# k'v with its operands swapped and two head pairs side by side in TensorE's columns, with other due times for the stages

## The chip, the cores and the metric

The kernel runs on one core of a Trainium2 chip. The metric is the device time of one execution in microseconds (us), here the median of several runs on the chip. The working views are those of one profiled execution: its page, its groups of instructions, its timeline, its windows of busy time and the chain of work that ended last.

## The reference, cut to what matters

Inputs are q, k and v of shape (4, 4, 1088, 32) (batch, heads, sequence, head dimension), two sketches S1 and S2 of shape (8, 32), and four weight matrices. The attention is linear, with 64 features for each head:

```python
def phi(x):                                   # r = 8, so 64 features
    a = einsum('rd,bhsd->bhsr', S1, x)
    b = einsum('rd,bhsd->bhsr', S2, x)
    return einsum('bhsi,bhsj->bhsij', a, b).reshape(..., 64)
q_p, k_p = phi(q), phi(k)
kv = einsum('bhsf,bhsd->bhfd', k_p, v)        # "k'v": 64 x 32 for each head
z = sum(k_p, axis=2)
x = (einsum('bhsf,bhfd->bhsd', q_p, kv) / (einsum('bhsf,bhf->bhs', q_p, z)[..., None] + 1e-06))
# then, with x as (batch, 1088, 128):
theta = x @ w_theta
y = einsum('ts,bsd->btd', w_tok_r, x * cos(theta)) + einsum('ts,bsd->btd', w_tok_i, x * sin(theta))
u = x + y
out = u + maximum(u @ w_ch, 0)
```

## The kernel before

The sequence is padded to nine chunks of 128 positions, in three groups of three chunks (`NG` = 3, `GC` = 3). Four batches go through the same stages, and each operation carries the name of its stage: `keysB` (loads, the k slices, sums for the denominators), `valuesB` (k features and k'v), `queriesB` (q slices, features, denominators), `mixedB` (numerators, the division, theta, cosine and sine) and `mixingB` (the token mixing with the two 1088 x 1088 matrices, the channel product and the output). The token matrices arrive as 64-bit words in 34 pieces of 544 columns (`w_tok` into `st`), and each piece is turned into float32 (`wT`) by three ScalarE activations (`step`, `step`, `wT`) and two VectorE operations (stage `weights`). These `wT` rows are the moving operands of every batch's mixing: 17 rows in three column groups of 384, 384 and 320, float32.

Nothing is issued in the order in which it is written. `Order.note` records every operation with an estimated duration, and `Order.lay_out` writes the orders of PE, DVE, ACT and SP out in advance: it walks a clock for each engine, takes among the operations that could start within `WAIT` of each other the one with the earliest due time, and allots the buffers. Due times run backwards from the ends; `SOONER` shifts them by stage (a negative number lets a stage come later), and the rows of the mixing get theirs from `START`, `PACE` and 0.65 a row. For PE the planner also follows a guess of the clock gate (an exponential average of PE's use, with two thresholds). Since all operations are issued from one helper, every instruction of the profile carries the same line (L319 before, L320 after), and they are told apart by the tiles they write and read. The engines themselves work through their written order and wait where an operand is late.

The step that is changed is `keys_values(b)`, stage `valuesB`. For each chunk and each pair of heads n it multiplies the k features of two heads (`kp` in the buffer `feat`, 128 positions x 128 features, the stationary operand) with the v of two heads (`vn` in a buffer `big`, 128 positions x 64, moving) and sums over the nine chunks in one PSUM bank, `kv[:, n]`, 128 features x 64. Two ScalarE copies then put the two diagonal blocks into `kvbd[b % 2]`, the block-diagonal operand of `numerator(b, g)`. In the profile each float32 product is two matmul instructions with two weight loads; k'v is the group `w<-big,feat`, 72 products and 144 instructions in all. The other names that matter: `fT` and `ks` (k or q features on their way), `ksl` and `qsl` (16-bit slices), `lv` (features for the denominators), `kvbd`, `xT`, `tn` and `tt` (mixed), `uT` and `ot` (output), `hmTq` (a small constant operand, used once early).

Of the kernel before, what the change touches and what calls it, by code (L numbers as in the profile page):

```python
# [32 lines left out]
P = 128  # L33
# [3 lines left out]
ROUND = 1.5 * 2.0**23  # L37
TWO_PI = 6.2831850
TINY = 2.0**-60
START = 90, 130, 170, 215  # L40
BIG = 5

SOONER = {"keys1": 20, "keys3": 15, "mixed0": 10, "mixed1": 20, "mixed3": 15, "mixing0": -20,
          "mixing1": -30, "mixing2": -25, "queries0": -5, "queries1": -5, "queries2": -10,
          "queries3": 5, "values1": 20, "values2": 25, "values3": 35}
ST = 6
PACE = 2.5
PIECE = 544
# [64 lines left out]
class Order:  # L113
# [3 lines left out]

    WAIT = 0.05  # L120

    def __init__(self, nc):
        self.nc, self.ops, self.due, self.tags, self.stage = nc, [], math.inf, {}, None
# [25 lines left out]
    def duration(self, engine, call, out, ins):  # L149

        n = math.prod(out.shape[1:])
        psum = any(isinstance(x, View) and x.buf.tag == "w" for x in ins)
        if engine == "DVE":
            if call == "tensor_reduce":
                n = math.prod(ins[0].shape[1:])
            if call == "reciprocal":
                return 0.29, 0.1
            own = any(isinstance(x, View) and x.shape[1:] == (1,) for x in ins[1:])
            fast = call in ("tensor_scalar", "tensor_copy", "memset") and not psum
            return 0.09 + n / (1920 if fast and not own else 1400 if fast else 970), 0.1  # L160
        if engine == "ACT":
            wide = any(isinstance(x, View) and x.buf.tag == "st" for x in ins)
            own = any(isinstance(x, View) and x.shape[1:] == (1,) for x in ins[1:])
            return 0.05 + 0.07 * own + n / (900 if out.dtype != F32 and wide else 1020 if wide else 1130), 0.15
        if engine == "SP":
            return 0.36, 0.0
        if call == "transpose":
            return 0.11, 0.3
        if ins[0].dtype == F32:
            return max(0.22, n / 600), 0.3  # L170
        return max(0.06, n / 2400), 0.3

    def note(self, engine, fn, call, a, kw):
# [38 lines left out]
    def lay_out(self):  # L212
        ops = self.ops
        self.dues()
        left, after = [len(op.behind) for op in ops], [[] for _ in ops]
        for op in ops:
            for n in op.behind:
                after[n].append(op.n)
        bufs = []
        for op in ops:  # L220
            for b in op.bufs:
                if b.uses[0] == op.n:
                    bufs.append(b)
        by_tag = {}
        for b in bufs:
            b.left = len(b.uses)
            by_tag.setdefault(b.tag, []).append(b)
        free = {tag: [0.0] * len(x[0].slots) for tag, x in by_tag.items()}
        waiting = {tag: list(x) for tag, x in by_tag.items()}
        live = {tag: [] for tag in by_tag}  # L230
        done = [False] * len(ops)

        def safe(b):

            if waiting[b.tag][0] is b:
                held = live[b.tag]
                if len(held) == 0:
                    return True
            events = []
            for x in live[b.tag] + [b]:  # L240
                events.append((max(n for n in x.uses if not done[n]), 1, -1))
            for x in waiting[b.tag]:
                if x is not b:
                    events += [(x.uses[0], 0, 1), (x.uses[-1], 1, -1)]
            count = len(live[b.tag]) + 1
            if count > len(b.slots):
                return False
            for _, _, d in sorted(events):
                count += d
                if count > len(b.slots):  # L250
                    return False
            return True

        clock = dict(PE=0.0, DVE=0.0, ACT=0.0, SP=0.0)
        ready = {e: [] for e in clock}
        at = [0.0] * len(ops)
        for op in ops:
            if not left[op.n]:
                ready[op.engine].append(op)
        link, use, used, slow = 0.0, 0.0, 0.0, True  # L260
        out, self.log = [], []
        while len(out) < len(ops):
            best = None
            for e, rs in ready.items():
                starts = []
                for op in rs:
                    t = max(clock[e], at[op.n])
                    for b in op.bufs:
                        if b.slot is None:
                            since = [x for x in free[b.tag] if x is not None]  # L270
                            t = max(t, min(since)) if since else math.inf
                    starts.append((t, op))
                while True:
                    first = min((t for t, _ in starts), default=math.inf)
                    if first == math.inf:
                        break
                    t, op = min(((t, o) for t, o in starts if t <= first + self.WAIT),
                                key=lambda x: (x[1].due, x[1].n))
                    if all(b.slot is not None or safe(b) for b in op.bufs):
                        if best is None or t < best[0]:  # L280
                            best = t, op
                        break
                    starts.remove((t, op))
            t, op = best
            e = op.engine
            for b in op.bufs:
                if b.slot is None:
                    b.slot = min((x, i) for i, x in enumerate(free[b.tag]) if x is not None)[1]
                    free[b.tag][b.slot] = None
                    waiting[b.tag].remove(b)  # L290
                    live[b.tag].append(b)
            cost = op.cost
            if e == "PE":
                use = use * math.exp(-(t - used) / 4.0)
                slow = use < (0.6 if slow else 0.3)
                cost *= 2.0 if slow else 1.0
                use, used = 1 - (1 - use) * math.exp(-cost / 4.0), t + cost
            end = clock[e] = t + cost
            if e == "SP":
                link = end = max(end + 1.6, link) + op.bytes / 290e3  # L300
            self.log.append((e, t, end, op))
            ready[e].remove(op)
            out.append(op)
            done[op.n] = True
            for b in op.bufs:
                b.left -= 1
                b.end = max(getattr(b, "end", 0.0), end + op.late)
                if not b.left:
                    free[b.tag][b.slot] = b.end
                    live[b.tag].remove(b)  # L310
            for n in after[op.n]:
                o = ops[n]
                at[n] = max(at[n], end if o.engine == e == "PE" else end + op.late)
                left[n] -= 1
                if not left[n]:
                    ready[o.engine].append(o)
        for op in out:
            r = [x.real() if isinstance(x, View) else x for x in op.args]
            op.call(*r, **{k: x.real() if isinstance(x, View) else x for k, x in op.kw.items()})  # L319
# [3 lines left out]
def kernel(  # L323
# [12 lines left out]
    B, _, NC, H, D = q.shape  # L336
# [113 lines left out]
    t_ = psum()  # L450
    T.transpose(t_[:2 * H, :P], View(hm.buf, hm.buf.slots[0]), ident)
    A.activation(hmT, t_[:2 * H, :P], AF.Copy, scale=512.0)
    hmTq = buf("hmTq", [P, P])[:H]
    t_ = psum()
    T.transpose(t_[:H, :P], hm, ident)
    A.activation(hmTq, t_[:H, :P], AF.Copy, scale=512.0)
# [81 lines left out]
    kvbd = []  # L538
# [139 lines left out]
    def keys_values(b):  # L678

        vn = tiles["v", b]  # L680
        kv = psum()[:, :4 * D].rearrange("p (n d) -> p n d", n=2)
        for g in range(NG):
            ks = tiles["kf", b, g]
            kp = buf("feat", [P, CH, R, R], F32, 2)
            tt(V, kp, ks[:, :, 0:R].unsqueeze(3).to_broadcast([P, CH, R, R]),
               ks[:, :, R:2 * R].unsqueeze(2).to_broadcast([P, CH, R, R]), ALU.mult)
            for i in range(GC):
                for n in range(2):
                    c = g * GC + i
                    T.matmul(  # L690
                        kv[:, n], kp[:, i * H + 2 * n:i * H + 2 * n + 2].rearrange("p h i j -> p (h i j)"),
                        vn[:, c, 2 * n:2 * n + 2].rearrange("p h d -> p (h d)"),
                        start=(c == 0 and n == 0), stop=(c == NC - 1), skip_group_check=True)
        for j in range(2):
            pj = slice(j * R * R, (j + 1) * R * R)
            A.copy(kvbd[b % 2][pj, :, j * D:(j + 1) * D], kv[pj, :, j * D:(j + 1) * D])


    NT = NC * HR
# [316 lines left out]
```

## Time and profile before

| | |
|---|---|
| median of 11 runs | 305.98 us (304.55 to 307.21) |
| the profiled execution | 305.75 us, its span 303.6 us |
| PE busy | 261.8 us (86%), 1347 matmuls |
| DVE busy | 227.1 us (75%) |
| ACT busy | 167.2 us (55%) |
| granted TensorE clock, mean | 0.906 |
| k'v, `w<-big,feat` | 144 matmuls, 20.7 us busy |

The page gives shares over the whole span, but the kernel has two parts: up to about 143 us the engines prepare batches and convert the token matrices, and afterwards PE works through the mixing. A share of the whole span therefore tells little; the windows and the chain do. Starts in the timeline matter more than the lengths of matmuls, since matmuls overlap: one float32 matmul of 64 columns is listed with 275 ns, while the next starts 112 ns after it.

### The profile page before, as it was taken

How to read it: one execution, taken by the hardware profiler on the slowest of the kernel's cores; microseconds unless marked ns; L12 is line 12 of the kernel's file. 1: busy time of each engine (PE TensorE's matmuls, PEld its weight loads, DVE VectorE, ACT ScalarE, POOL GpSimd, SP SyncE). 2: the span in 40 equal slices, each digit the busy share in tenths (PEclk: the TensorE clock that was granted, in tenths of full speed). 3: DMA queues.
4: the chain of work that ended last, by engine and by line, in shares of the span. 5: the costliest groups of instructions: out<-in, count | busy, mean ns of one | idle time of the engine just before them, and what ended most of it. 6: DMA issues, size and time to landing. Idle time of an engine off the chain costs nothing.

```text
span 303.6 us, 4008 instructions
## 1 busy us (share of the span) xinstructions
PE 261.8 (86%) x1347; PEld 188.3 (62%) x1347; DVE 227.1 (75%) x646; ACT 167.2 (55%) x334; POOL 0.7 (0%) x6
## 2 busy tenths in 40 slices
PE   4739688743987999488999999999999999999993
PEld 3528576533874656256966676687668766666661
DVE  5999897989699898999999894999789752000121
ACT  4696647598479999999864315325934162000000
POOL 0000000000000000000000000000000000000000
PEclk9958758785597999869999999999999999999998
DMA  7980456658001476752200001000100000000011
GB/s 271 408 339 2 166 189 188 212 154 287 0 2 54 125 266 189 276 201 73 80 1 0 2 26 28 1 1 22 28 26 2 22 0 26 2 0 26 2 46 48
DMA packets 11603, 28.77 MB, mean 95 GB/s; under 512 B 1216, under 2 KB 5568, under 8 KB 11584
## 3 DMA queue, kind: packets, MB, share of 16 engines
q1 hardware_dynamic: 11584, 28.53, 27.6%
q8 instruction: 10, 0.16, 0.2%
q14 instruction: 9, 0.07, 0.1%
HBM read 26.30 MB, written 2.23 MB: 94 GB/s over the span
## 4 chain that ended last, share of the span: by engine, by line
PE 68%; ACT 16%; DVE 10%; DMA 3%; issue 1%; ACTq 0%; DVEq 0%
PE w L319 68%; ACT step L319 7%; ACT wT L319 3%; ACT big L319 2%; ACT lv L319 2%; DMA st<-w_tok 2%; DVE big L319 1%; DMA big<-k_l 1%; DVE wT L319 1%; ACT fT L319 1%; DVE feat L319 1%; DVE m L319 1%; DVE cut_r L319 1%; DVE cut_z L319 1%; DVE ksl L319 0%
## 5 line engine op out<-in xcount | busy, mean ns | idle before, releaser
L319 PE MATMUL w<-wT,st 128*128 128x384 f32 (+1 forms) x384 | 134.2, 482 | 5.0 <-DVE st L319 2.5
L319 PEld LDWEIGHTS w<-wT,st 128*128 128x128 f32 x384 | 68.8, 194 | 38.8 <-DVE wT L319 4.4
L319 ACT ACTIVATE step<-st 128x544 f16<-128x544 f32 (+2 forms) x70 | 53.1, 799 | 2.7 <-DVE wT L319 2.7
L319 ACT COPY ot<-w 128x384 f32<-128x384 f32 (+2 forms) x16 | 6.0, 396 | 55.6 <-PE w L319 55.6
L319 ACT COPY fT<-w 128x256 f32<-128x256 f32 (+1 forms) x48 | 18.3, 398 | 30.9 <-PE w L319 30.8
L319 PE MATMUL w<-ident,feat 128*128 128x128 f32 x72 | 15.9, 311 | 11.9 <-ACT step L319 8.1
L319 PEld LDWEIGHTS w<-kvbd,fT 128*128 128x128 f32 x144 | 22.4, 222 | 4.6 <-ACT fT L319 3.7
L319 PE MATMUL w<-kvbd,fT 128*128 128x64 f32 x144 | 23.5, 297 | 1.5 <-ACT fT L319 1.4
L319 DVE CUSTOM_DVE_ANT_0 wT<-wT,step 128x1088 uint16<-128x1088 uint16 x34 | 24.1, 715 | 0.6 <-ACT step L319 0.6
L319 DVE SCALAR_TENSOR_TENSOR uT<-w,uT 128x384 f32<-128x384 f32 (+1 forms) x12 | 6.4, 532 | 23.1 <-PE w L319 23.0
L319 ACT ACTIVATE wT<-st 128x544 f32<-128x544 f32 x34 | 23.0, 687 | 0.2
L319 PE MATMUL w<-big,feat 128*128 128x64 f32 x144 | 20.7, 284 | 1.8 <-DVE feat L319 1.8
L319 DVE TENSOR_TENSOR uT<-xT,w 128x384 f32<-128x384 f32 (+1 forms) x12 | 6.3, 529 | 21.2 <-PE w L319 21.1
L319 PEld LDWEIGHTS w<-big,feat 128*128 128x128 f32 x144 | 19.8, 205 | 3.2 <-DVE feat L319 2.3
L319 PEld LDWEIGHTS w<-ident,feat 128*128 128x128 f32 x72 | 10.9, 175 | 15.9 <-ACT step L319 8.1
L319 ACT COPY lv<-w 128x384 f32<-128x384 f32 x36 | 15.9, 488 | 4.6 <-PE w L319 4.3
L319 PE MATMUL w<-mv,qsl 128*128 128x384 f16 (+2 forms) x108 | 18.0, 301 | 0.0
L319 PE MATMUL w<-ksl 128*128 128x384 f16 x72 | 16.0, 369 | 0.0
L319 PEld LDWEIGHTS <-qsl 128*128 128x128 f16 x108 | 11.1, 106 | 7.7 <-issue 3.4
L319 PE MATMUL w<-ident,big 128*128 128x128 f32 x72 | 12.9, 332 | 2.3 <-DMA big<-k_l 2.3
L319 DVE TENSOR_SCALAR wT<-wT 128x544 int32<-128x544 int32 x34 | 14.4, 432 | 0.6 <-ACT wT L319 0.4
L319 PEld LDWEIGHTS w<-ident,big 128*128 128x128 f32 x72 | 10.9, 181 | 3.2 <-DMA big<-k_l 2.8
(187 smaller groups left out, 409.5 us busy)
## 6 DMA issues: line engine op xcount, KB each, us to landing
st<-w_tok SPq DMA_DIRECT2D x34, 544.0 KB, 4.6
big<-k_l SPq DMA_DIRECT2D x4, 576.0 KB, 4.0
big<-q_l SPq DMA_DIRECT2D x4, 576.0 KB, 3.8
big<-v_l SPq DMA_DIRECT2D x4, 576.0 KB, 5.0
out<-ot SPq DMA_DIRECT2D x8, 192.0 KB, 2.1
out<-ot SPq DMA_DIRECT2D x4, 128.0 KB, 1.8
st<-w_sq SPq DMA_DIRECT2D x1, 256.0 KB, 3.8
out<-ot SPq DMA_DIRECT2D x4, 32.0 KB, 1.8
```

The costliest lines, as they stand in the source:

```text
L319: op.call(*r, **{k: x.real() if isinstance(x, View) else x for k, x in op.kw.items()})
```

## The change

In `keys_values` the operands change places. v of a head pair (64 columns) becomes the stationary operand and the features (128 columns) the moving one, so the sum is v'k, 64 x 128 for each pair; pair 0 goes to columns 0 to 63 of TensorE's array and PSUM partitions 0 to 63, pair 1 to columns 64 to 127 and partitions 64 to 127 (`tile_position`). At the end of a batch the 128 x 128 sum is copied to SBUF (`kvt`, which shares its buffer with `hmTq`), transposed by TensorE into another bank, and from there the two copies into `kvbd` are as before. The planner is told that a float32 product with a stationary operand of up to 64 columns takes half the time; its guess of the clock gate gets a longer memory (6 in place of 4) and higher thresholds (0.75 and 0.5 in place of 0.6 and 0.3), `WAIT` falls to 0.03, and `SOONER` and `START` have other numbers. So the whole written order is another one.

```diff
-START = 90, 130, 170, 215
+START = 95, 130, 170, 215
...
-SOONER = {"keys1": 20, "keys3": 15, "mixed0": 10, "mixed1": 20, "mixed3": 15, "mixing0": -20,
-          "mixing1": -30, "mixing2": -25, "queries0": -5, "queries1": -5, "queries2": -10,
-          "queries3": 5, "values1": 20, "values2": 25, "values3": 35}
+SOONER = {"keys1": 20, "keys3": 10, "mixed0": 10, "mixed1": 15, "mixed2": 20, "mixing0": -25,
+          "mixing1": -35, "mixing2": -15, "mixing3": -10, "queries0": -25, "queries1": -5,
+          "queries2": -10, "queries3": -5, "values0": -5, "values1": 10, "values2": 15,
+          "values3": 35}
...
-    WAIT = 0.05
+    WAIT = 0.03
...
-            return max(0.22, n / 600), 0.3
+            return max(0.22, n / 600) / (1 if ins[0].shape[1] > 64 else 2), 0.3
...
-                use = use * math.exp(-(t - used) / 4.0)
-                slow = use < (0.6 if slow else 0.3)
+                use = use * math.exp(-(t - used) / 6.0)
+                slow = use < (0.75 if slow else 0.5)
...
-    hmTq = buf("hmTq", [P, P])[:H]
+    hmTq = buf("kvt", [P, P])[:H]
...
-        kv = psum()[:, :4 * D].rearrange("p (n d) -> p n d", n=2)
+        kv = psum()[:, :P]
...
-                    T.matmul(
-                        kv[:, n], kp[:, i * H + 2 * n:i * H + 2 * n + 2].rearrange("p h i j -> p (h i j)"),
-                        vn[:, c, 2 * n:2 * n + 2].rearrange("p h d -> p (h d)"),
-                        start=(c == 0 and n == 0), stop=(c == NC - 1), skip_group_check=True)
+                    T.matmul(kv[n * 2 * D:(n + 1) * 2 * D], vn[:, c, 2 * n:2 * n + 2].rearrange("p h d -> p (h d)"),
+                             kp[:, i * H + 2 * n:i * H + 2 * n + 2].rearrange("p h i j -> p (h i j)"),
+                             start=(c == 0), stop=(c == NC - 1), tile_position=(0, n * 2 * D), skip_group_check=True)
+        kvt = buf("kvt", [P, P])
+        A.copy(kvt, kv)
+        t = psum()[:, :P]
+        T.transpose(t, kvt, ident)
+        t = t.rearrange("p (n d) -> p n d", n=2)
         for j in range(2):
             pj = slice(j * R * R, (j + 1) * R * R)
-            A.copy(kvbd[b % 2][pj, :, j * D:(j + 1) * D], kv[pj, :, j * D:(j + 1) * D])
+            A.copy(kvbd[b % 2][pj, :, j * D:(j + 1) * D], t[pj, :, j * D:(j + 1) * D])
```

More of the change, by code (lines that the diff above doesn't have):

```diff
@@ L261, in lay_out @@
         out, self.log = [], []
-        while len(out) < len(ops):
+        while len(self.log) < len(ops):
             best = None
@@ L293, in lay_out @@
             if e == "PE":
-                use = use * math.exp(-(t - used) / 4.0)
-                slow = use < (0.6 if slow else 0.3)
+                use = use * math.exp(-(t - used) / 6.0)
+                slow = use < (0.75 if slow else 0.5)
                 cost *= 2.0 if slow else 1.0
-                use, used = 1 - (1 - use) * math.exp(-cost / 4.0), t + cost
+                use, used = 1 - (1 - use) * math.exp(-cost / 6.0), t + cost
             end = clock[e] = t + cost
```

## The prediction

> **What bounds the kernel now.** I read the windows first, since a share of the whole span mixes two parts. Columns: the stretch, then busy time of PE, weight loads, DVE and ACT with counts, the granted clock, the DMA share and GB/s.
>
> ```profile
> 0.00:100.00 100.00, 70.05 (x411) 57.43 (x412) 87.97 (x306) 69.57 (x138) 0.70 (x6) 0.76 0.49 174
> 100.00:142.80 42.80, 35.92 (x158) 22.55 (x156) 39.65 (x73) 41.53 (x76) 0.00 (x0) 0.92 0.59 197
> 142.80:297.30 154.50, 154.49 (x774) 107.77 (x774) 98.52 (x267) 55.53 (x120) 0.00 (x0) 1.00 0.06 17
> 297.30:303.60 6.30, 1.35 (x5) 0.58 (x5) 0.98 (x2) 0.53 (x2) 0.00 (x0) 0.79 0.20 52
> ```
>
> From 142.8 us PE never rests and has the full clock; before that DVE is busy 127.6 of 142.8 us, ACT full from 100 on, and PE waits for them. The chain of waits (start, length, what) says the same:
>
> ```profile
> 142.38 0.38 ACT fT L319
> 142.81 154.50 PE w L319 x774
> 297.33 0.50 DVE uT L319
> ```
>
> So the end is the time at which PE stops waiting, plus the PE work that is left then, plus about 6 us of tail that the change leaves alone. Next, the groups by form (busy, mean ns, idle before), for what changes:
>
> ```profile
> L319 PE MATMUL w<-big,feat 128*128 128x64 f32 x144 | 20.7, 284 | 1.8 <-DVE feat L319 1.8
> L319 PE MATMUL w<-w,xT 128*128 128x128 f32 x72 | 9.4, 276 | 0.0
> L319 ACT COPY kvbd<-w 64x64 f32<-64x64 f32 x8 | 1.6, 204 | 6.0 <-PE w L319 5.9
> L319 ACT COPY ks<-w 128x192 f32<-128x192 f32 x12 | 3.6, 314 | 4.8 <-PE w L319 2.6 <-DVE tz L319 1.3 <-DVE feat L319 0.9
> ```
>
> These means overlap. What a matmul costs is the distance between starts, from the timeline of PE:
>
> ```profile
> 25.19 1.45 PE L319 MATMUL w<-big,feat 128*128 128x64 f32 x12
> 26.47 1.06 PE L319 MATMUL w<-s_bd,fT 128*128 128x64 f32 x8
> ...
> 34.75 2.82 PE L319 MATMUL w<-big,feat 128*128 128x64 f32 x12 [0.79 <-DVE feat L319]
> 37.36 2.15 PE L319 MATMUL w<-ident,big 128*128 128x128 f32 x9
> ...
> 49.42 0.38 PE L319 MATMUL w<-dgn,ones 1*128 1x4 f32 x2
> 49.73 0.66 PE L319 MATMUL w<-big,feat 128*128 128x64 f32 x4
> ...
> 209.35 0.49 PE L319 MATMUL w<-ident,uT 128*128 128x128 f32 x3
> 209.68 0.70 PE L319 MATMUL w<-wT,st 128*128 128x320 f32 x2
> ```
>
> Twelve k'v instructions take 26.47 - 25.19 = 1.28 us at full clock (0.107 each; the median over all is 0.112) and 37.36 - 34.75 = 2.61 at half clock (0.22). By the same reading a float32 instruction with 128 moving columns takes 0.112 too (`w<-w,xT`), a transpose 0.109, a mixing instruction 0.323 (384 columns) or 0.269 (320). With these the PE work of the whole kernel is 234.6 us; of the 303.6 us of span 69 are waiting, half clock and tail, 62 of them gone by 142.8.
>
> **The change, part by part.** *k'v itself.* 144 x 0.112 = 16.1 us become, if the two column halves run at the same time, 72 x 0.112 = 8.1; the moving side is now 128 columns, which the `w<-w,xT` row prices at the same 0.112 an instruction. Four transposes add 0.4. PE's work falls by 7.6 to 227.0 us. Nothing in this trace uses two column halves at once, so the price per instruction lies between 0.056 (paired) and 0.112 (no pairing), and, if the load of 64 weight columns no longer hides behind a matmul, half a load more, 0.167. I take 0.056, because each half has its own columns and PSUM partitions; the other ends go into the range.
>
> The Trainium skill ("TensorE: Matmul & The Clock Gate", Packing small matmuls) states 2.38x measured for three column tiles, an efficiency of 0.79; by an estimate from that, two tiles give 1.59x, and the saving would be 6.0 us in place of 8.1. No run here shows it.
>
> *Switching between whole array and halves.* k'v stands in 23 runs in the new order. The 32-row matmuls show what a switch can cost: two `dgn,ones` take 49.73 - 49.42 = 0.31 us where two ordinary ones take 0.22, so 0.09 is for leaving; the first of them starts 0.205 after the matmul before it in place of 0.112, 0.09 for entering, less what the smaller matmul saves: together some 0.16. The 64-column transposes show the other end: the third of the three at 209.35 has 64 columns, and all three take 0.33 us, 0.11 each, no switch to be seen. So the bounds are 0 and 23 x 0.16 = 3.7 us, four of the runs in the second part. I take 0, the nearer row, as it is columns that are halved.
>
> The Trainium skill ("TensorEngine Tiling (Array Packing)", Tiling Modes) says that changing the mode drains TensorE, which speaks against the change; by it the 3.7 us would be due in full. The 32-row rows agree with it and the 64-column row does not.
>
> *The new tail of k'v.* A copy of 128 x 128 (between the rows of 0.204 and 0.314, so 0.25), a transpose and the old two copies: 0.9 us more from the last product to `kvbd`, in each batch. In the new order the numerators that read it come 44, 34, 14 and 22 us of ACT's queue later, so it hides; on ACT the mixed stage's activations queue behind the copy, on PE `s_bd` products or mixing rows stand between the sum and its transpose. If a transpose came too soon, PE would wait up to 0.9 us four times.
>
> *Where the PE saving lies.* Of the 144 instructions 72 run by 65 us and 12 between 120 and 142.8, where PE also waits for others; 60 are behind 142.8, on the path. So 60 x 0.056 = 3.4 us are sure; the rest counts only if PE does something else in the freed time. The new order shows that: I compare the state at the last `step` activation of the token matrices, in the trace at 151.4 us. Behind it PE has 146.7 us of work in the old order: with it the trace would end at 298.1, and PE's last instruction does end at 299.8. In the new order 139.8 are left: 6 mixing products fewer (-3.7), 18 k'v products at 0.112 for 19 at 0.224 (-2.2), three products and three transposes of mixed1 fewer (-1.0), the rest even. So -6.9.
>
> *Other due times.* Against that, ACT has more queued in front of that `step`: seven more activations and a copy of mixed1 and two `kvt` copies, less one `fT` copy, nine more in balance, 4.2 us of listed time. They overlap by 0.1 each, as these rows show (starts 0.49 and 0.42 apart, lengths 0.59 and 0.51):
>
> ```profile
> 151.24 0.59 ACT L319 ACTIVATE tn<-tn,halfpi 128x384 f32<-128x384 f32 x1
> 151.73 0.51 ACT L319 ACTIVATE tt<-tt 128x384 f32<-128x384 f32 x1
> 152.15 0.41 ACT L319 COPY kvbd<-w 64x64 f32<-64x64 f32 x2
> ```
>
> So the `step` comes 3.3 us later, and the sum is 3.3 - 6.9 = -3.6. DVE's queue in front of its last `wT` operation grows by 3.2 us listed and PE's work behind that falls from 141.2 to 136.3, which says the same within 2 us. The loads on SP keep their place among the pieces within a few pieces, and the DMA share of 0.5 leaves room.
>
> *Early waits for PE.* ACT idles 30 us in the first 100. Three k'v runs stand just in front of such waits: 12 instructions at 25.19 (0.7 to save), 12 at half clock at 34.75 (1.3), 22 from 48.48 (1.2). All would be 3.2 us; other runs stand there now, and copies and transposes come in, so I take a third, 1.1, with +1 and -3.2 as bounds.
>
> Sum: 305.75 - 3.6 - 1.1 = 301.1 us, against the profiled execution; the median is 0.2 above it. A difference of 0.3%, 0.9 us, is about what a measurement of this kernel tells from none.
>
> **The rivals.** *More is gained*: the early waits go in full and ACT's longer queue is swallowed by its idle time: 305.75 - 7.6 - 3.2 = 295.0. For it speak the 30 us of idle ACT; against it DVE, 88% busy up to 142.8. *The halves do not run together*: k'v costs what it did, PE has 2.0 us more behind the `step`, the early waits stay: 305.75 + 3.3 - 4.9 = 304.2, and up to 308 with switches of 0.16. *The clock gate closes where PE is dense in the first part* (slower): the clock was full from 96.1 to 126.8, with 30.7 us; it was at half from 65.4 to 82.5, with PE busy 9.6 of those 17.1 us, and again from 126.8 to 133.7. In the new order PE has 24 us of work in the part of ACT's queue that covers this, as before some 25, but less of it is k'v and it comes 10 us of PE work earlier in the stream, so it sits nearer to the edge. If half of the stretch runs at half clock, 7.7 us of PE work are left for later: 301.1 + 7.7 = 308.8. It decides from 9.4 us of extra half clock, which eat the gain of 4.7.
>
> **How the numbers follow.** Forecast 0.42, more gained 0.13, no pairing 0.20 (0.07 faster, 0.05 the same, 0.08 slower), the gate 0.25. Faster 0.62, the same 0.05, slower 0.33. The range runs from 296.0, leaving out the best of the second case, to 309.0, the price of the gate.
>
> **What would show it.** k'v starts in pairs, 12 instructions in about 0.67 us; PE without rest from about 139 to 145 us on, with some 140 us of work behind the last `step`, which should end near 153 to 155; the mean clock not below 0.90. If 12 k'v instructions still take 1.3 us, pairing is wrong; if the last `step` ends after 159, the queue term is; if new stretches of half clock appear after 85 us, the gate rival holds.

## The result and the profile after

The changed kernel takes 303.04 us (median of 12 runs, 301.22 to 303.82) against 306.12 for the kernel before on the same chips; the ratio is 0.989, with a 95% interval of 0.987 to 0.991. The profiled execution took 303.24 us, with a span of 301.1 and a mean granted clock of 0.905. Four slow executions, at a lower mean clock, are left out of the medians below: one of the new order with the old k'v (309.14 us) and three of the run with all the planner's numbers (311.4 to 311.8).

The windows of the kernel after, with the columns as before (busy PE, weight loads, DVE, ACT, POOL, then clock, DMA share, GB/s):

```profile
0.00:100.00 100.00, 65.19 (x380) 48.99 (x381) 87.92 (x308) 70.11 (x137) 0.70 (x6) 0.73 0.55 197
100.00:142.80 42.80, 40.51 (x230) 28.55 (x229) 41.20 (x78) 40.11 (x78) 0.00 (x0) 1.00 0.42 134
142.80:294.78 151.98, 151.91 (x739) 101.28 (x737) 96.74 (x262) 56.29 (x124) 0.00 (x0) 1.00 0.07 20
```

PE does less in the first 100 us (65.2 us busy in place of 70.1) and is nearly without rest already between 100 and 142.8 (40.5 us busy in place of 35.9). The chain of waits shows it too:

```profile
106.06 0.57 DVE tt L320
...
106.67 92.69 PE w L320 x500
...
294.78 0.50 DVE uT L320
```

The last wait of PE on another engine, apart from the tail, ends at 106.7 us, and no longer at 142.8. Now k'v, in the groups by form and in PE's timeline:

```profile
L320 PE MATMUL w<-feat,big 128*64 128x128 f32 x144 | 15.4, 295 | 0.0
L320 ACT COPY kvt<-w 128x128 f32<-128x128 f32 x4 | 1.0, 262 | 0.0
```

```profile
61.24 0.43 PE L320 MATMUL w<-feat,big 128*64 128x128 f32 x2
61.60 0.30 PE L320 MATMUL w<-mv,qsl 128*128 128x288 f16 x1
...
107.13 0.88 PE L320 MATMUL w<-feat,big 128*64 128x128 f32 x12
107.93 0.88 PE L320 MATMUL w<-s_bd,fT 128*128 128x64 f32 x6
```

From start to next start, six products (12 instructions) take 107.93 - 107.13 = 0.80 us. Single starts in the trace show the pairs: two matmuls 6 or 7 ns apart, the next two 103 to 109 ns later; after the first pair 160. The matmul before a run is followed only after 0.205 us where 0.112 is usual, and the one behind the run starts 0.202 to 0.205 after the last matmul in place of 0.109. So at full clock a run costs 0.109 for every pair, and 0.24 more whatever its length: 0.09 on entering, 0.05 behind the first pair, 0.09 on leaving. A product that stands alone has no partner, and its two matmuls start one after the other: it takes 0.36 (61.60 - 61.24), as long as two products, plus the 0.09 for entering. In the kernel before, six products took 1.28 to 1.29 at full clock and a single one 0.17 to 0.25.

At full clock the 23 runs of the changed kernel, 11 of them with a single product, come by these lengths to 14.9 us, where the 72 products took 16.1.

Theory A, from this: products pair as hoped, but each run pays 0.24 us, and in 23 runs that eats most of the saving; the gain of the whole must then come from the other written order. Theory B is the prediction's: the swap brings it.

### The profile page after: what moved, and what is told of

Read it like the earlier page. It is cut to its first block, busy times and chain, and to the rows that moved or that the text cites. A ratio compares the mean times of both kernels' runs of the same rounds, so it can differ in the third digit from the quotient of the medians.

```text
span 301.1 us, 4002 instructions
## 1 busy us (share of the span) xinstructions
PE 259.0 (86%) x1351; PEld 179.4 (60%) x1351; DVE 226.8 (75%) x646; ACT 167.0 (55%) x338; POOL 0.7 (0%) x6
## 4 chain that ended last, share of the span: by engine, by line
PE 78%; DVE 13%; ACT 3%; DMA 3%; issue 2%; ACTq 0%; DVEq 0%
PE w L320 78%; DMA big<-k_l 3%; DVE big L320 2%; DVE wT L320 2%; ACT step L320 1%; DVE m L320 1%; DVE cut_r L320 1%; ACT big L320 1%; DVE feat L320 1%; DVE fl L320 1%; DVE cut_z L320 1%; ACT lv L320 0%; DVE ksl L320 0%; DVE mx L320 0%; DVE lv L320 0%
## 5 line engine op out<-in xcount | busy, mean ns | idle before, releaser
L320 PE MATMUL w<-wT,st 128*128 128x384 f32 (+1 forms) x384 | 130.9, 473 | 0.0
L320 PEld LDWEIGHTS w<-wT,st 128*128 128x128 f32 x384 | 67.7, 190 | 32.0 <-issue 2.8
L320 PE MATMUL w<-mv,qsl 128*128 128x192 f16 (+2 forms) x108 | 21.8, 323 | 8.2 <-DVE mv L320 6.0
L320 ACT COPY lv<-w 128x384 f32<-128x384 f32 x36 | 16.6, 485 | 17.2 <-PE w L320 16.9
L320 PE MATMUL w<-s_bd,fT 128*128 128x64 f32 x72 | 13.3, 318 | 4.9 <-DVE pw L320 4.4
L320 PE MATMUL w<-ident,big 128*128 128x128 f32 x72 | 14.0, 332 | 2.6 <-DMA big<-k_l 2.6
L320 PEld LDWEIGHTS w<-s_bd,fT 128*128 128x128 f32 x72 | 11.3, 224 | 6.9 <-DVE pw L320 4.6
L320 PE MATMUL w<-feat,big 128*64 128x128 f32 x144 | 15.4, 295 | 0.0
```

## The experiments

The first two runs cross the two halves of the change: each written order with the other form of k'v. The written order is kept instruction by instruction, and only what is issued in its places is replaced.

**Old order, swapped k'v.**

```diff
-                    T.matmul(kv[:, n], kp[..], vn[..], start=(c == 0 and n == 0), ...)
+                    o = T.matmul(kv[:, n], kp[..], vn[..], ...)            # planned as before
+                    o.instead = matmul(bank[n * 2 * D:(n + 1) * 2 * D, :P], vn[..], kp[..],
+                                       start=(c == 0), tile_position=(0, n * 2 * D), ...)
...
+        # in the place of the kvbd copies: copy into hmTq's buffer, transpose into the same bank,
+        # and, up to four ACT operations later, the two kvbd copies
```

> The written order of the kernel before, instruction by instruction, with k'v swapped into the two column halves in place (plus the copy, the transpose and the two copies at the end of each batch). Theory A (products pair, but each run of k'v costs 0.24 us for entering and leaving the halves, and a product that stands alone costs as much as two): behind 142.8 us the old order has 15 runs of 3, 1, 1, 1, 6, 1, 1, 1, 1, 1, 1, 1, 5, 1 and 5 products, 8.4 us in place of 6.1, and two transposes: about 306.1 + 2.5 = 308.6 us. Theory B (the swap halves the PE work, as the prediction had it): 60 instructions save 0.056 each, 302.7 us.

Measured: 309.46 us, ratio 1.011 (1.008 to 1.015). The swap alone makes the kernel slower, by somewhat more than theory A said. PE's timeline of this run shows why:

```profile
173.94 0.43 PE L339 MATMUL w<-feat,big 128*64 128x128 f32 x2
174.31 0.34 PE L339 MATMUL w<-ksl 128*128 128x384 f16 x1
...
175.51 0.91 PE L339 MATMUL w<-uT,w 128*128 128x384 f32 x2
```

The same stretch of the kernel before:

```profile
171.97 0.33 PE L319 MATMUL w<-big,feat 128*128 128x64 f32 x2
172.14 0.33 PE L319 MATMUL w<-ksl 128*128 128x384 f16 x1
...
172.75 0.86 PE L319 MATMUL w<-uT,w 128*128 128x384 f32 x2
```

Three products of k'v (the third is left out here) and two matmuls of `ksl` between them take 172.75 - 171.97 = 0.78 us before and 175.51 - 173.94 = 1.57 with the halves: three entries and three exits for three products. Of the 3.3 us over the kernel before, theory A's lengths give 2.5; a wait of PE for `kvbd` behind 142.8 us, which the kernel before does not have, gives 0.4. Theory B fails (it said 302.7).

**New order, old k'v.**

```diff
-                    T.matmul(kv[n * 2 * D:(n + 1) * 2 * D], vn[..], kp[..], tile_position=(0, n * 2 * D), ...)
+                    o = T.matmul(kv[n * 2 * D:(n + 1) * 2 * D], vn[..], kp[..], ...)   # planned as in the change
+                    o.instead = matmul(kv2[:, n], kp[..], vn[..], start=(c == 0 and n == 0), ...)
...
+        # in the place of the kvt copy the two kvbd copies from PSUM; no transpose
```

> The written order of the changed kernel with k'v as before: old operands, no kvt copy and no transpose, the two kvbd copies in the place of the kvt copy. From 100 us on PE is dense there, with 36 products in 8 runs. Theory A: swapped these cost 6.3 us, unswapped 8.0, less 0.3 for three transposes: 303.0 + 1.4 = 304.4 us, so that most of the gain belongs to the other order. Theory B: 36 products x 0.112 less 0.3: 306.8 us, the gain belongs to the swap.

Measured: 303.87 us, ratio 0.992 (0.989 to 0.995). So of some 3 us the other order brings about 2.3 by itself. The swap brings some 0.8 on top, which the times alone do not tell from nothing: the intervals of the two ratios overlap, and a second set of the changed kernel, further down, took 303.55. In the chain PE runs from 106.05 us on without a wait, as in the changed kernel, with k'v unchanged:

```profile
106.05 188.82 PE w L323 x935
```

From there to the end of PE's last matmul this kernel takes 191.3 us (to 297.4), and the changed kernel 190.6 (106.7 to 297.3). So in the two traces the swap is worth 0.7 us behind this point, where theory A had 1.4.

Counting PE's work at full-clock distances between starts, as the prediction does, the kernel before has lost 63 us by 150 us to waits and half clock and loses hardly more until 290; this one has lost 60.3. That is the order's gain, with the same 234.6 us of work; which of the many moved operations bring it is not shown.

**Fewer runs of k'v.** In the changed kernel the six products of each group of chunks are moved to the place of the last one.

```diff
+        # o.group = (b, g), o.place = (i, n) for each k'v product
+        # on issuing: a product waits for the last of its group, then all six in the order of place
```

> The changed kernel, the six products of each group of chunks moved to the place of the last of them, so that k'v stands in 12 runs and not in 23; nothing else moved. Theory A: behind 100 us 6 runs in place of 8, 5.4 us in place of 6.3: 302.1 us, every run about 0.8 us and none of 0.36. Theory B (a switch costs nothing): 303.0, no change.

Measured: 302.26 us, ratio 0.986 (0.983 to 0.990); all twelve runs last 0.805 to 0.808 us. A second time, beside the changed kernel on the same chip:

> The changed kernel as it is, for a comparison on the same chip with the gathered one: about 303.0 us.

> The gathered kernel once more beside the changed one. Theory A: two runs of k'v fewer in the dense part, 6 runs in place of 8, 0.9 us less than the changed kernel: about 302.2 us. If the earlier distance was between chips: the same time as the changed kernel.

Measured: changed kernel 303.55 us (303.18 to 303.91), gathered kernel 301.45 (299.88 to 301.80), ratios to the kernel before 0.991 (0.988 to 0.994) and 0.983 (0.979 to 0.987). The two sets of runs do not overlap, and the gathered kernel is the fastest of all that ran. It was 0.8 us ahead of the change once and 2.1 the second time, where 0.9 was expected. That the first number fits is luck, as the traces show. The 0.9 was to come from the dense part, but there the gathered kernel has a wait of PE that the changed kernel does not have, since the run that stood at 108.80 was moved away:

```profile
108.34 0.38 ACT lv L327
108.72 0.17 issue
108.89 5.08 PE w L327 x17
```

Between the last `s_bd` product and 108.89 PE is idle for 0.50 us. From the `qsl` matmuls just ahead of the first k'v run of the dense part to its end PE takes 190.6 us in the changed kernel and 190.4 in the gathered one, and 190.4 in both the second time. The rest of the lead is there before: these matmuls start 0.4 us sooner once (106.25 for 106.67) and 3.7 the second time (103.69 for 107.36). In that first part two executions of one kernel lie as far apart: 0.7 us for the changed kernel, 2.6 for the gathered one. So the runs show that the gathered kernel is faster, but not that fewer switches in the dense part are the reason.

**Is it the pairing?**

```diff
-    o.place = (i, n)        # left half, right half, left half, ...
+    o.place = (n, i)        # three products left, then three right
```

> As the run with gathered groups, but within each group the three products of the left half first, then the three of the right half, so that neighbours share a half. If it is the pairing of neighbours in different halves that makes a run short (theory A), a run grows from 0.8 to about 1.4 us, six of them behind 100 us: 302.1 + 3.4 = 305.5 us. If a run is short for another reason (the smaller weight load alone), its length stays at 0.8 and the time at 302.1.

Measured: 303.61 us, ratio 0.992 (0.989 to 0.995), every run of six at full clock 1.074 to 1.076 us:

```profile
146.85 1.15 PE L327 MATMUL w<-feat,big 128*64 128x128 f32 x12
147.93 1.45 PE L327 MATMUL w<-wT,st 128*128 128x320 f32 x4
```

It lies between the two expectations. Neighbours in different halves do matter (0.27 us for each run, 1.6 for the six behind 100 us, against 1.35 measured), so a smaller weight load is not what shortens a run. The dense part of the trace grows as much as the time, from 190.4 us to 191.7. But 1.4 was too much. The trace does not name the half of a matmul; the twelve starts fall into two rows with the spacing of a single half, 0, 160, 269, 378, 487 and 597 ns, and 275, 436, 545, 654, 763 and 872. Read so, PE begins with the right half while three left-half matmuls that stand before it are still to start, and only the delay of the second row is lost, 275 ns in place of 6.

**What in the planner brings the order's gain?** The planner's numbers, with k'v as before and planned at its old cost: all of them, the due times alone, the clock gate's guess and `WAIT` alone.

```diff
-START = 90, 130, 170, 215
+START = 95, 130, 170, 215
...                                     # and SOONER as in the change: first and second run
-                use = use * math.exp(-(t - used) / 4.0)
-                slow = use < (0.6 if slow else 0.3)
+                use = use * math.exp(-(t - used) / 6.0)
+                slow = use < (0.75 if slow else 0.5)
...                                     # and WAIT = 0.03: first and third run
```

> The kernel before with k'v and its planned cost as they were, and all the other planner numbers of the change: START, SOONER, WAIT, the memory and thresholds of the clock gate. The planner writes its own order from them. Theory D (these numbers bring the gain, whatever k'v costs): about 303.9 us, as the new order with the old k'v gave. Theory L (the numbers were fitted to one order, and another planned cost of k'v leads elsewhere): 306 us or more, with no gain over the kernel before.

> The kernel before with START and SOONER of the change alone. Theory D with the due times as the part that counts: about 304 us. If the planner's gate and WAIT are what counts: 306. Theory L: anywhere from 303 to 310.

> The kernel before with WAIT, the memory and the thresholds of the planner's clock gate of the change alone. Theory D with the gate as the part that counts: about 304 us. If the due times count: 306. Theory L: anywhere from 303 to 310, since the old due times were fitted to the old gate.

Measured: 306.12 (ratio 1.001, 0.998 to 1.004), 307.84 (1.007, 1.004 to 1.010) and 312.11 us (1.021, 1.017 to 1.024). None has the gain; the first differs from the run with the new order and the old k'v only in what the planner was told of k'v (its cost, the copy and the transpose), and is 2.3 us slower. By the same count of lost time they stand at 64, 68 and 69 us by 160 us, where PE has become dense; the profiled execution of the second was 2.6 us over its median. So none of these sets of numbers brings the gain without the planned cost that it was written with; which operations' places make it stays open.

**The planner with whole groups.** The six products are recorded as one operation with its measured length.

```diff
-            for i in range(GC): for n in range(2): T.matmul(...)
+            order.note("PE", products, "group", (kv, vn[:, g * GC:(g + 1) * GC], kp, g), {})
...
+        if call == "group":
+            return 0.9, 0.3
```

> The changed kernel with the six products of a group recorded as one operation of 0.9 us, the length that a run of six has been seen to take with its entry, so that the planner writes an order with 12 runs by itself. By theory A the PE work is that of the gathered run: 302.3 us if the order is as good. By theory L the order is another one and the time lies anywhere from 300 to 306.

Measured: 312.73 us, ratio 1.023 (1.020 to 1.026), the slowest of all, though k'v stands in only 9 runs (at full clock 0.81 us for one group and 1.46 for two; three runs fell into half clock and take 1.48 to 1.91). PE still waits for others between 143 and 169 us, and the clock is at half once more from 150.9 to 157.7:

```profile
149.73 0.44 PE L322 MATMUL w<-ident,feat 128*128 128x128 f32 x2 [0.52 <-ACT fT L322]
...
162.83 0.94 PE L322 MATMUL w<-w,xT 128*128 128x128 f32 x6 [0.84 <-ACT xT L322]
```

**A small step of one number.**

```diff
-START = 95, 130, 170, 215
+START = 94, 130, 170, 215
```

> The changed kernel with the first number of START at 94 in place of 95, one microsecond of one due time. Theory L (the time belongs to one written order, and the planner's numbers only pick it): another order, and the time moves by more than 1 us either way from 303.0. Theory D (the numbers stand for a real preference in time): within 0.5 us of 303.0.

Measured: 303.64 us, ratio 0.991 (0.988 to 0.994), the same as the changed kernel beside it, though the written order differs in many places. So theory L is too strong as it stood: not every other order is another time. A microsecond in a due time did nothing; another planned cost of k'v moved the time by 2.3 us, the gate and `WAIT` by 5.8, the group by 9.7. Nor is it PE's early density by itself that makes the time, for in this run's chain PE still waits up to 140.5 us, about as in the kernel before:

```profile
140.46 155.24 PE w L320 x765
```

## Why the prediction was right and where it was not

It forecast 301.1 us, and the kernel takes 303.0: faster, by 3.1 us in place of 4.7. The number came out, the share of each half of the change did not.

*The time of the last weight conversion held.* It was to come 3.3 us later in ACT's queue, less 1.1 for early waits: 153.6 us. It ends at 153.7 (the split into the 3.3 and the 1.1 was not tested):

```profile
152.88 0.83 ACT L320 ACTIVATE step<-st 128x544 int16<-128x544 uint32 x1
153.55 0.27 ACT L320 COPY kvt<-w 128x128 f32<-128x128 f32 x1
```

*The PE work behind it was too small.* From there PE needs until 297.26, so 143.5 us, where the kernel before needed 148.4 from its own `step`: 4.9 less, and not 6.9. These 2.0 us, and the 0.1 of the `step`, are the whole miss of the profiled execution (303.24 against 301.1). The step that failed is the price of a switch. The prediction gave the bounds 0 and 0.16 a run and took 0 from the 64-column transposes, because they are halved columns too. k'v pays like the 32-row matmuls, and the 0.05 behind the first pair besides. Four runs behind the `step` were priced at 2.0 us and take 3.1: 0.8, 0.8, 0.8 and 0.36, with 0.09 for each entry. This accounts for 1.1 of the 2.1; the rest was not pinned down.

The Trainium skill ("TensorEngine Tiling (Array Packing)", Tiling Modes), that changing the mode drains TensorE, agrees with the runs of k'v: they cost 0.24 us in and out. By it the prediction would have had 3.7 us of switches.

With the measured price the 23 runs pay 23 x 0.24 = 5.5 us, which is most of the 7.6 us that were to be saved.

*The pairing was right*: 0.109 for two instructions, and a run of six, entry included, takes 0.90 in place of 1.28 (the sign that was set, 12 instructions in about 0.67, left out the 0.24). That a product alone has no partner was not in the prediction.

*The credit was wrong.* The sum took the swap as the source of the gain and the other order as its price. The crossed runs show the opposite: in the old order the swap costs 3.3 us, in the new one it gives at most some 0.8, and the new order alone gives 2.3. The sum came out near because it counted what is left behind a mark in the new order, and that contains both; as an account of the swap it was luck. Reading the 26 and 23 runs of k'v beside the 32-row price would have been a warning.

*The rivals.* That the halves do not run together is refuted. The clock gate did not take more than before: half clock adds up to 55 us up to 142.8 in either kernel, where the rival needed 9.4 us more. Its sign, half clock behind 85 us, did show: one stretch lasts up to 100.3, where the kernel before had half clock from 92.7 to 96.1 only, but the stretch from 126.8 to 133.7 is gone. In the kernel after most of the half clock is that one stretch (window and chain):

```profile
69.60:100.30 30.70, 20.54 (x90) 16.83 (x91) 27.42 (x77) 22.55 (x43) 0.00 (x0) 0.50 0.47 168
```

```profile
78.63 12.70 PE w L320 x59
...
91.75 5.04 PE w L320 x20
```

There PE is on the path for 17.7 us at half clock, so the gate costs something in this kernel too; from 100.3 on the clock is full. "PE without rest from 139 to 145" was too late, it is from 106.7; the mean clock held, 0.905. The four new tails of k'v are hidden as said: nobody waits for `kvt`, and one `kvbd` copy waits 0.3 us.

## What to carry to other kernels

A small matmul in part of the array is not priced by its own length: count the runs between full-array matmuls, price entry and exit, and keep such products together (here six together give 0.90 us in place of 1.28, one alone costs 0.45 in place of about 0.2). When a change moves both the work and the written order, cross them, old order with new work and new order with old work, before giving either the credit. A planner's costs and due times belong together: a truer cost of one step (the group of 0.9 us) gave an order 3% slower than the changed kernel's, while the same grouping done by hand in the written order made the kernel the fastest of the series.

## What the runs showed of the hardware that was not expected

Transposes with 64 columns pass between full-array matmuls without any switch (0.109 from start to start), while k'v with 64 columns pays 0.24 a run; both are listed with 128*64 in the profile, so the size alone does not tell. And matmuls of the two halves seem not to start strictly in the written order: with three products left and three right, a second row of starts with the spacing of one half begins 275 ns into the run, ahead of three left-half matmuls that stand before it. The trace does not name the halves, so this is read from the spacing.
